# Chunk 0's score masking shared out between ScalarE, GpSimd and VectorE in a gated-linear-attention plus MLP kernel

## The chip, the core and the metric

The kernel runs on one core of a Trainium2 chip. A core has five engines that each work through their own list of instructions in order: TensorE (PE in the profile; its weight loads are shown apart as PEld), VectorE (DVE), ScalarE (ACT), GpSimd (POOL) and SyncE (SP, which here only issues DMAs). They wait for each other through semaphores. Matmul results land in PSUM, of which this kernel uses six banks of 512 numbers per partition and two tiles of sums; VectorE and ScalarE read them there, and GpSimd is given operands in SBUF only. The metric is the device time of one execution in microseconds, lower is better.

## The reference

```python
for t in range(S):                                   # q, k, v, alpha: (4, 8, 768, 48)
    state = alpha[:, :, t, :, None] * state + np.einsum('bhd,bhe->bhde', k[:, :, t], v[:, :, t])
    y[:, :, t] = np.einsum('bhd,bhde->bhe', q[:, :, t], state)
x = y.transpose(0, 2, 1, 3).reshape(B, S, H * D)     # (4, 768, 384)
xn = (x - mean(x)) / sqrt(var(x) + 1e-6) * g_ln      # over the last axis
out = x + maximum(xn @ w_ch1, 0) @ w_ch2             # 384 -> 1536 -> 384
```

A recurrence over 768 steps with a decaying 48x48 state per head is followed by a normalisation and a two-layer perceptron. All of it is single precision.

## The kernel before, in words

The sequence of each of the 4 batch entries is cut into 6 chunks of 128 steps. For one chunk of one entry (one "turn letter": a, b, c, d are chunk 0 of entries 0 to 3, e to h chunk 1, and so on to x) `attention(c, b)` does the following in pieces: logarithm of the gates (L296), running sums by a matmul with a triangle (L300), exponentials of both signs (L307, L308), scaled keys and queries (L314, L317), then transposes. In chunk 0 the transposes are matmuls (L334) whose results ScalarE copies out of PSUM (L338), queries first and keys second. The scores are matmuls (L368) with keys on the partitions and queries along the free axis, into two banks of 4 heads each, 128x512. They have to be masked: a key may only serve a query that is not earlier. Before the change VectorE does that with two `copy_predicated` per entry (L383), which write to the tile `at` only where the triangle `mask` is not zero; `at` was cleared beforehand. There are two tiles `at`, one for the even and one for the odd entries. The masked scores then meet the values (L427), beside the chunk's sum of outer products (L401) that becomes the state (L412). The outputs are summed and normalised on ScalarE: L454 copies them out of PSUM with their sum, L472 to L476 work out mean and spread, L478 and L479 apply them, L485 (PE) transposes, L489 (ACT) copies the result to `xT0`.

For chunk 0 the perceptron runs in plain single precision: first layer L520 on PE and L523 on ACT, two entries at a time, second layer L534. It needs the normalised rows of entries a and b (both L489) and the weights. In this data set the weights arrive as 64-bit numbers, and `take_weights` turns each of 12 pieces into single precision in VectorE and ScalarE steps: L186, L188, L190 (DVE), L194 (ACT, which waits for L190), L196 and L200 or L203 (DVE, which wait for L194). For the later chunks the weights are split in two parts (L213 to L219), and the products run as three cheaper ones (L557, L564, L623).

Nothing decides at run time what comes next. The string `ORDER` has one letter for each piece of each generator (a piece ends at a `yield`): a to x are the attention turns, A to L the weight pieces, Y and Z the first layer of chunk 0, and so on. Reading it from left to right gives each engine its list of instructions, and each engine keeps to its list. An instruction whose input isn't there holds up all that stands behind it on its engine.

```python
with tc.manual_schedule():
    for turn in ORDER:
        next(turns[turn], None)
```

Of the kernel before, what the change touches and what calls it, by code (L numbers as in the profile page):

```python
# [17 lines left out]
AFT = mybir.ActivationFunctionType  # L18
AOP = mybir.AluOpType
# [7 lines left out]
LOW = 2.0 ** -12  # L27

ORDER = (
    "NNNabaMMMNaaaaWVcbbbMccaaaabbbbbVccaaabbdcccbccddAAdWadaAaadbcccdbVbbBWVaaaddaabWNdccddb"  # L30
    "bbCbacddBBDVbbcCCddcddddeddYYDDYYYYeYWcccYcWWddYYEYYYYccYENNNFFEMWOF%ZWZeZZZZeZGZZZZZZZe"
    "eeGHYHGZZZZZZZZYMYYYZY%IeZWIHgeWJIfYWYYPJJg!Vffffee?OfffgeeKQ(LKMKMLL*gggOO#e.g!&fQQQQQQ"
    "?!!h+Q)eefege#eef&fffhhe.PPff(eNQQ%g//V#hh#eNe&eefffff&ieeffM+hhhf*PPPfffP*)ggggiiif%+PV"
    "M+j?i?ii-11211P((21133))gg1422-3i5P441115/h11523423N5N43gg5hhhhh4667-66ikk5gg6Vghh..gggg"
    "h*hiihhhhhhO-Ojii/MNji6jjjjj77ggk7h7Mggh7hh888881111821mmkkk3kjk2231131O444551122O113425"
    "Vll573366j66445iiii5N66ijjjjjk7ViijMkjlllliikkkkkjjj7iijjjjllii7ij7jjVnlmjmmN718888111Mm"
    "22m88111133442231554k5onkkmkkllllll2kkkk111OOm73V233N444M5566k66576lknnnnllnolll6mnmmm77"
    "ookklllllll88877V11pp188N111o223311n44M55OmO22mmmm33n4m5mm4666nnnpp57omm1112mnn12poo33n4"
    "4566m856nnnnVnn777npmmmnnVon88pnn7788111118223314qNM12N5N211334445N2oooqooqpp55q11q66ooo"
    "r23oo4opppp7pp1M6Mppp563oooo4566poqq8qoorrppp7o77pppVpp7pOV7Orrrrr118s888882123u1111142q"  # L40
    "34356115123445q66252qqqqq3sNss13tt46rqqqssqq4rrrVrrrqqqqM7tssrr556O6rqq7rrrrrOqu7qvtt7tt"
    "strrrr7r711888V881121112M334223N5sssvss14455ssss3ssuutttttss7458uusuu1t66t111wNs26233445"
    "5tt7MMO666stttt8tVt7V7ttsOtt88t7ss788vvvvO11111v122133x24211153344455u51166622336uuuu4ww"
    "vO478u55uuvuuvvvv67uuuV6vvwwwuwvvMvvv7vv7uuuuvvvv77w888xxxx88V11111122xx33O2314441155122"
    "5x3311263644ww64wwww7555ww66wwxxxxxwwwwxx7xx6xx7xxx7wxxxxOOwww7788888811111221O133442231"
    "31142555112663364447555866677777888888"
)


# [1 line left out]
def kernel(  # L51
# [17 lines left out]
    nc = tc.nc  # L69
# [4 lines left out]
    P = 128  # L74
    NCB = S // P
    NP = H // 2
# [39 lines left out]
    act, ts = nc.scalar.activation, nc.vector.tensor_scalar  # L116
    stt = nc.vector.scalar_tensor_tensor

    def rd(x):
        return x.bitcast(F32R)  # L120

    HS = P // 2
# [4 lines left out]
    mask, mask_of_halves = tri.bitcast(INT32), consts[:, 2 * P:].bitcast(INT32)  # L127
    nc.gpsimd.memset(consts[:, :2 * P], 1.0)
    nc.gpsimd.affine_select(out=tri, in_=tri, pattern=[[1, P]], base=0, channel_multiplier=-1,
                            compare_op=AOP.is_ge, fill=0.0)  # L130
    nc.gpsimd.affine_select(out=ident, in_=ident, pattern=[[1, P]], base=0, channel_multiplier=-1,
                            compare_op=AOP.is_equal, fill=0.0)
# [3 lines left out]
    def at_first(name, then):  # L136
# [20 lines left out]
    hh, hl, hs = (hid[:, i * NJ * HB * P:][:, :NJ * HB * P].rearrange(  # L157
        "p (j b t) -> p j b t", b=HB, t=P) for i in range(3))
# [131 lines left out]
    def attention(c, b):  # L290
        whole, last = c == 0, c + 1 == NCB
# [34 lines left out]
        at = ats[b % len(ats)]  # L326
        if not whole:
            at = at_parts[b % len(ats)][0].rearrange("k (p s t) -> k p s t", s=2, t=HS)
# [13 lines left out]
        else:  # L342
            nc.vector.transpose(out=tr.rearrange("t n i p d -> t (n i p) d"),
                                in_=qk.rearrange("t n i p d -> t (n i p) d"))
# [35 lines left out]
        give_kq(kT)  # L380
        yield
        for i, scores in enumerate(aps):
            nc.vector.copy_predicated(  # L383
                out=at[:, :, i].rearrange("k p s t -> k p (s t)") if whole else
                at.rearrange("k p s t -> k (p s) t"),
                data=scores.rearrange("k p s t -> k p (s t)" if whole else "k p s t -> k (p s) t"),
                mask=mask.unsqueeze(1).broadcast_to([P, NP, P]) if whole else
                mask_of_halves.unsqueeze(1).broadcast_to([P, 2 * NP, HS]))
            give_bank(scores)
        yield  # L390
        gate = gate_tile(P, 2, NP)
        with nc.allow_non_contiguous_dma(reason="two rows to columns"):
            nc.sync.dma_start(gate[:, :ne], line[:ne].rearrange("o (p r) -> r o p", p=NP))
# [248 lines left out]
    turns = {"YZ"[h]: first_of_chunk_0(h) for h in range(2)}  # L642
    turns |= {"PQ"[h]: second_of_chunk_0(h) for h in range(2)}
    turns |= {chr(ord("a") + n): attention(n // B, n % B) for n in range(NCB * B)}
    turns |= {t: take_weights(i) for i, t in enumerate("ABCDEFGHIJKL")}
    turns |= {t: split_weights(i) for i, t in enumerate("!#?%&()*+-./")}
# [35 lines left out]
```

## Time and profile before

| | |
|---|---|
| median of 3 runs | 405.09 us (404.27 to 408.36) |
| the profiled execution | 405.11 us, of it 403.4 us span of the core |
| TensorE busy | 396.5 us of the span (98%) |
| VectorE busy | 264.5 us (66%) |
| ScalarE busy | 251.2 us (62%) |
| GpSimd busy | 121.6 us (30%) |
| copy_predicated, all 28 (8 of them chunk 0's, 128x512 each) | median 732 ns |

How to read it: an engine at 98% leaves the question of where its other 2% are, and what stands behind them. The view by windows tells busy time stage by stage, the chain of waits tells what released what, and the timeline gives single instructions with their start, length and, in brackets, the idle time ahead of them with the engine and line that ended it. A name such as L338 is a line of the kernel before; `x2` behind a row means that two equal instructions were merged into it.

### The profile page before, as it was taken

How to read it: one execution, taken by the hardware profiler on the slowest of the kernel's cores; microseconds unless marked ns; L12 is line 12 of the kernel's file. 1: busy time of each engine (PE TensorE's matmuls, PEld its weight loads, DVE VectorE, ACT ScalarE, POOL GpSimd, SP SyncE). 2: the span in 40 equal slices, each digit the busy share in tenths (PEclk: the TensorE clock that was granted, in tenths of full speed). 3: DMA queues.
4: the chain of work that ended last, by engine and by line, in shares of the span. 5: the costliest groups of instructions: out<-in, count | busy, mean ns of one | idle time of the engine just before them, and what ended most of it. 6: DMA issues, size and time to landing. Idle time of an engine off the chain costs nothing.

```text
span 403.4 us, 12267 instructions
## 1 busy us (share of the span) xinstructions
PE 396.5 (98%) x5000; PEld 366.8 (91%) x5000; DVE 264.5 (66%) x468; ACT 251.2 (62%) x562; POOL 121.6 (30%) x129
## 2 busy tenths in 40 slices
PE   8999999999999999999999999999999999999996
PEld 6778886667999999999999999999999999999996
DVE  4898999989996665564564665575563664661461
ACT  5797655688884755674673774773575566556440
POOL 3010000023462442082352362352064171152170
PEclk9999999999999999999999999999999999999999
DMA  7888787767747837565456637748547715533101
GB/s 229 247 264 286 253 200 222 195 155 166 184 127 180 198 116 168 107 189 104 144 114 209 112 103 165 170 109 175 134 85 231 165 29 135 130 64 99 59 2 39
DMA packets 134240, 61.15 MB, mean 152 GB/s; under 512 B 90876, under 2 KB 130300, under 8 KB 134184
## 3 DMA queue, kind: packets, MB, share of 16 engines
q1 hardware_dynamic: 134184, 60.37, 58.9%
q8 instruction: 39, 0.64, 0.7%
q14 instruction: 17, 0.14, 0.1%
HBM read 42.95 MB, written 17.39 MB: 150 GB/s over the span
## 4 chain that ended last, share of the span: by engine, by line
PE 96%; ACT 1%; DVE 1%; issue 0%; DVEq 0%
PE bank L623 32%; PE bank L564 20%; PE bank L557 10%; PE bank L520 8%; PE bank L534 8%; PE bank L375 4%; PE bank L432 3%; PE sums L401 2%; PE bank L435 2%; PE bank L485 2%; PE bank L230 1%; PE bank L284 1%; PE bank L368 1%; PE bank L300 1%; PE bank L427 1%; PE bank L334 0%
## 5 line engine op out<-in xcount | busy, mean ns | idle before, releaser
L610 POOL TENSOR_TENSOR hid<-hid 128x512 fp32r<-128x512 f32 x60 | 76.1, 1291 | 63.9 <-DVE hid L602 59.7
L564 PE MATMUL bank<-xh,w1h 128*128 128x256 f32 x360 | 85.2, 278 | 0.0
L564 PE MATMUL bank<-xl,w1l 128*128 128x256 f32 x360 | 84.8, 276 | 0.0
L623 PE MATMUL bank<-w2h,hid 128*128 128x384 f32 x240 | 83.0, 346 | 0.0
L623 PE MATMUL bank<-w2l,hid 128*128 128x384 f32 x240 | 80.6, 336 | 0.0
L576 ACT ACTIVATE at<-bank 128x512 f32<-128x512 f32 x60 | 36.2, 604 | 60.3 <-PE bank L557 58.9
L584 DVE SCALAR_TENSOR_TENSOR bank<-bank,at 128x512 f32<-128x512 f32 x60 | 41.5, 696 | 41.5 <-PE bank L564 35.8
L564 PEld LDWEIGHTS bank<-xh,w1h 128*128 128x128 f32 x360 | 67.6, 188 | 0.2
L564 PEld LDWEIGHTS bank<-xl,w1l 128*128 128x128 f32 x360 | 67.6, 188 | 0.0
L557 PE MATMUL bank<-xs,ws 128*128 128x256 f32 x360 | 50.9, 277 | 0.0
L557 PEld LDWEIGHTS bank<-xs,ws 128*128 128x128 f32 x360 | 46.1, 188 | 0.3
L623 PEld LDWEIGHTS bank<-w2h,hid 128*128 128x128 f32 x240 | 45.1, 188 | 0.6
L623 PE MATMUL bank<-ws,hid 128*128 128x384 f32 x240 | 45.4, 336 | 0.0
L602 DVE SCALAR_TENSOR_TENSOR hid<-bank,hid 128x512 fp32r<-128x512 f32 x60 | 39.7, 683 | 8.5 <-ACT hid L594 8.2
L623 PEld LDWEIGHTS bank<-w2l,hid 128*128 128x128 f32 x240 | 45.1, 188 | 0.2 <-DVE hid L602 0.2
L419 POOL TENSOR_TENSOR mid<-mid,gate 112x192 f32<-112x192 f32 x20 | 11.0, 552 | 107.9 <-DMA kqT<-td 50.2
L623 PEld LDWEIGHTS bank<-ws,hid 128*128 128x128 f32 x240 | 41.6, 188 | 0.2
L593 ACT ACTIVATE hid<-bank 128x512 fp32r<-128x512 f32 x60 | 36.3, 605 | 8.3 <-DVE bank L584 8.0
L500 POOL TENSOR_TENSOR xs<-xs,xl 128x384 fp32r<-128x384 f32 x20 | 21.4, 1078 | 53.9 <-DVE xl L497 53.9
L594 ACT ACTIVATE hid<-bank 128x512 fp32r<-128x512 f32 x60 | 36.7, 611 | 0.0
L520 PE MATMUL bank<-early_hid,w 128*128 128x256 f32 x144 | 32.1, 382 | 0.0
L534 PE MATMUL bank<-w,early_hid 128*128 128x384 f32 x96 | 32.1, 489 | 0.0
(101 smaller groups left out, 784.7 us busy)
## 6 DMA issues: line engine op xcount, KB each, us to landing
early_w2l<-in_moe_w_ch_dram SPq DMA_DIRECT2D x12, 768.0 KB
td<-tr SPq DMA_DIRECT2D x80, 96.0 KB
kqT<-td SPq DMA_DIRECT2D x80, 96.0 KB
row<-in_alpha_dram SPq DMA_DIRECT2D x24, 192.0 KB
qk<-in_k_dram SPq DMA_DIRECT2D x24, 192.0 KB
qk<-in_q_dram SPq DMA_DIRECT2D x24, 192.0 KB
vn<-in_v_dram SPq DMA_DIRECT2D x24, 192.0 KB
kept<-row SPq DMA_DIRECT2D x24, 192.0 KB
```

Source lines behind the costliest of these rows:

```text
L500: nc.gpsimd.tensor_sub(rd(diff), diff, low)
L520: nc.tensor.matmul(hps, pieces[j // 2][0][:, f, j % 2 * P:][:, :P], xT0[:, f, bs], start=(f == 0), stop=(f == NF - 1))
L534: nc.tensor.matmul(ops, hT0[:, j, b], wholes[NT + j // 2][:, j % 2], start=(j == 0), stop=(j == NJ - 1))
L557: nc.tensor.matmul(hpb[:, i], rd(wj[i * NF + f][2]), rd(xv[f][2]), start=(f == 0), stop=(f == NF - 1))
L564: nc.tensor.matmul(hpa[:, i], rd(wj[i * NF + f][e]), rd(xv[f][e]), start=(f == 0 and e == 0), stop=(f == NF - 1 and e == 1))
L576: act(out=negs[t % len(negs)], in_=hpb, func=AFT.Copy, scale=-1.0)
L584: stt(out=z, in0=z, scalar=1 + LOW, in1=negs[t % len(negs)], op0=AOP.mult, op1=AOP.add)
L593: act(out=rd(high), in_=z, func=AFT.Relu, scale=1 - LOW / 2)
L594: act(out=rd(diff), in_=z, func=AFT.Relu, scale=LOW * (1 - LOW / 2))
L602: stt(out=rd(low), in0=z, scalar=0.0, in1=high, op0=AOP.max, op1=AOP.subtract)
L610: nc.gpsimd.tensor_sub(rd(diff), diff, low)
L623: nc.tensor.matmul(acc, rd(x[:, j, i]), rd(of[k][:, j % 2]), start=j == 0 and k != 1, stop=j == NJ - 1 and k != 0)
```

## The change

In chunk 0 the scores of an entry are treated by halves of the queries (HS is 64). The first 64 queries can only see the first 64 keys, so ScalarE copies that 64x64 corner of each head, unmasked, from PSUM to `at` (two instructions per entry, each 64 partitions by 4x64). GpSimd then clears what lies on the wrong side of the diagonal, with one `affine_select` per entry on 64x8x64 elements in SBUF. VectorE's `copy_predicated` stays for the other 64 queries, two per entry, each 128x4x64 in place of 128x4x128. The later chunks are as before.

```diff
-    "NNNabaMMMNaaaaWVcbbbMccaaaabbbbbVccaaabbdcccbccddAAdWadaAaadbcccdbVbbBWVaaaddaabWNdccddb"
+    "NNNabaMMMNaaaaWVcbbbMccaaaabbbbbVccaaabbdcccbccddAAdWadaAaadbccccdbVbbBWVaaaddaabWNdcc"
...
         for i, scores in enumerate(aps):
+            if whole:
+                act(out=at[:HS, :, i, 0], in_=scores[:HS, :, 0], func=AFT.Copy)
             nc.vector.copy_predicated(
-                out=at[:, :, i].rearrange("k p s t -> k p (s t)") if whole else
-                at.rearrange("k p s t -> k (p s) t"),
-                data=scores.rearrange("k p s t -> k p (s t)" if whole else "k p s t -> k (p s) t"),
-                mask=mask.unsqueeze(1).broadcast_to([P, NP, P]) if whole else
+                out=at[:, :, i, 1] if whole else at.rearrange("k p s t -> k (p s) t"),
+                data=scores[:, :, 1] if whole else scores.rearrange("k p s t -> k (p s) t"),
+                mask=mask[:, HS:].unsqueeze(1).broadcast_to([P, NP, HS]) if whole else
                 mask_of_halves.unsqueeze(1).broadcast_to([P, 2 * NP, HS]))
             give_bank(scores)
         yield
+        if whole:
+            first = at[:HS].rearrange("k p i s t -> k (p i) s t")[:, :, 0]
+            nc.gpsimd.affine_select(out=first, in_=first, pattern=[[0, 2 * NP], [1, HS]], base=0,
+                                    channel_multiplier=-1, compare_op=AOP.is_ge, fill=0.0)
+            yield
```

The new `yield` gives each chunk-0 turn one piece more. ORDER gets one letter more for each of a, b, c and d, right behind the piece that masks, so that all other pieces keep their places; nothing moves on PE or SP. In the changed file the new lines are L384 (the copy), L385 (copy_predicated) and L394 (the selection), and each line behind them has a number higher by 6.

On ScalarE, in the stretch of entries a and b (kqT_85 and kqT_86 are first a's and then c's transposed queries and keys, kqT_87 and kqT_88 are b's, at_175 belongs to a and at_176 to b), the list changes like this:

```order
 L338 COPY kqT_86<-bank_71 112x512
 L338 COPY kqT_87<-bank_66 112x512
+L384 ACTIVATE at_175<-bank_68 64x4x64
+L384 ACTIVATE at_175<-bank_70 64x4x64
 L338 COPY kqT_88<-bank_67 112x512
 L296 ACTIVATE row_75<-row_75 128x384
 L338 COPY kqT_85<-bank_69 112x512
+L384 ACTIVATE at_176<-bank_71 64x4x64
+L384 ACTIVATE at_176<-bank_66 64x4x64
 L338 COPY kqT_86<-bank_68 112x512
```

The copies of a's scores now stand between the copy of b's queries and the copy of b's keys, and those of b's scores between c's queries and c's keys.

On ScalarE a little later, where b's output is normalised, the changed kernel has these rows (L460 is L454 of before; kqT_88 is now entry d's keys, at_176 takes d's scores; L478 to L485 are L472 to L479 of before, for entry b):

```order
L460 ACTIVATE row_72,few_96<-bank_68 128x384
L338 COPY kqT_88<-bank_70 112x512
L384 ACTIVATE at_176<-bank_69 64x4x64
L384 ACTIVATE at_176<-bank_71 64x4x64
L478 ACTIVATE few_96<-few_96 128x1
L479 ACTIVATE row_74,few_96<-row_72,few_96 128x384
```

Before, L472 stood right behind the copy to kqT_88; now the two copies of d's scores stand between them, and d's scores can only be computed once kqT_88 is there.

On VectorE the changed kernel's masking of a and b, with the engines on whose semaphores each row waits:

```order
L385 COPY_PREDICATED at_175<-consts,bank_68 128x4x64 [waits Activation_49,Pool_49]
L385 COPY_PREDICATED at_175<-consts,bank_70 128x4x64 [waits Activation_49]
L385 COPY_PREDICATED at_176<-consts,bank_71 128x4x64 [waits PE_49,Activation_49]
L385 COPY_PREDICATED at_176<-consts,bank_66 128x4x64 [waits PE_49,Activation_49]
L186 TENSOR_SCALAR w_122<-early_w2l 128x768 [waits DMAHW3_49]
```

The masking instructions keep their place on VectorE, ahead of the first weight piece, and their lists of waits name ScalarE (Activation), which now reads the same bank ahead of them.

More of the change, by code (lines that the diff above doesn't have):

```diff
@@ L29 @@
 ORDER = (
-    "NNNabaMMMNaaaaWVcbbbMccaaaabbbbbVccaaabbdcccbccddAAdWadaAaadbcccdbVbbBWVaaaddaabWNdccddb"
[L31 to L46, printed above, removed]
+    "NNNabaMMMNaaaaWVcbbbMccaaaabbbbbVccaaaabbdcccbbccddAAdWadaAaadbccccdbVbbBWVaaaddaabWNdcc"
@@ new lines @@
+    "dddbbbCbacddBBDVbbcCCddcddddeddYYDDYYYYeYWcccYcWWddYYEYYYYccYENNNFFEMWOF%ZWZeZZZZeZGZZZZ"
+    "ZZZeeeGHYHGZZZZZZZZYMYYYZY%IeZWIHgeWJIfYWYYPJJg!Vffffee?OfffgeeKQ(LKMKMLL*gggOO#e.g!&fQQ"
+    "QQQQ?!!h+Q)eefege#eef&fffhhe.PPff(eNQQ%g//V#hh#eNe&eefffff&ieeffM+hhhf*PPPfffP*)ggggiiif"
+    "%+PVM+j?i?ii-11211P((21133))gg1422-3i5P441115/h11523423N5N43gg5hhhhh4667-66ikk5gg6Vghh.."
+    "ggggh*hiihhhhhhO-Ojii/MNji6jjjjj77ggk7h7Mggh7hh888881111821mmkkk3kjk2231131O444551122O11"
+    "3425Vll573366j66445iiii5N66ijjjjjk7ViijMkjlllliikkkkkjjj7iijjjjllii7ij7jjVnlmjmmN7188881"
@@ new lines @@
+    "11Mm22m88111133442231554k5onkkmkkllllll2kkkk111OOm73V233N444M5566k66576lknnnnllnolll6mnm"
+    "mm77ookklllllll88877V11pp188N111o223311n44M55OmO22mmmm33n4m5mm4666nnnpp57omm1112mnn12poo"
+    "33n44566m856nnnnVnn777npmmmnnVon88pnn7788111118223314qNM12N5N211334445N2oooqooqpp55q11q6"
+    "6ooor23oo4opppp7pp1M6Mppp563oooo4566poqq8qoorrppp7o77pppVpp7pOV7Orrrrr118s888882123u1111"
+    "142q34356115123445q66252qqqqq3sNss13tt46rqqqssqq4rrrVrrrqqqqM7tssrr556O6rqq7rrrrrOqu7qvt"
+    "t7ttstrrrr7r711888V881121112M334223N5sssvss14455ssss3ssuutttttss7458uusuu1t66t111wNs2623"
@@ L47 @@
+    "34455tt7MMO666stttt8tVt7V7ttsOtt88t7ss788vvvvO11111v122133x24211153344455u51166622336uuu"
+    "u4wwvO478u55uuvuuvvvv67uuuV6vvwwwuwvvMvvv7vv7uuuuvvvv77w888xxxx88V11111122xx33O231444115"
+    "51225x3311263644ww64wwww7555ww66wwxxxxxwwwwxx7xx6xx7xxx7wxxxxOOwww7788888811111221O13344"
+    "223131142555112663364447555866677777888888"
 )
```

## The prediction, made before the changed kernel was run

> **What bounds the kernel now.** I read the page first: TensorE's share and its row of slices.
>
> ```profile
> span 403.4 us, 12267 instructions
> ...
> PE 396.5 (98%) x5000; PEld 366.8 (91%) x5000; DVE 264.5 (66%) x468; ACT 251.2 (62%) x562; POOL 121.6 (30%) x129
> ...
> PE   8999999999999999999999999999999999999996
> ```
>
> A tenth of the span is 40 us, a digit 10 us. TensorE is full from the fourth digit on; what it lacks lies at the two ends. The view by windows shows the front end in us:
>
> ```profile
> 10.00:20.00 10.00, 9.42 (x167) 7.83 (x165) 8.64 (x16) 7.35 (x19) 0.00 (x0) 1.00 0.89 246
> 20.00:30.00 10.00, 9.21 (x138) 7.80 (x138) 9.79 (x18) 9.20 (x26) 1.05 (x2) 1.00 0.80 270
> ...
> 80.00:240.00 160.00, 160.00 (x2403) 151.31 (x2396) 107.84 (x194) 107.99 (x242) 61.24 (x62) 1.00 0.63 150
> ```
>
> Columns are the window, its length, then busy us of PE, PEld, DVE, ACT and POOL. From 10 to 30 us PE lacks 1.37 us, while VectorE and ScalarE are close to full; from 80 to 240 us PE lacks nothing. The view of waits, for PE alone from 60 us to the end, has a single row:
>
> ```profile
> PE sums L401 <- issue: 0.2, 1, 0.2
> ```
>
> So once PE has begun its dense run it waits for nobody, and the kernel's time is the time at which that run begins, plus a fixed length. What sets the beginning is in the chain of waits (start, length, what):
>
> ```profile
> 15.74 0.57 DVE early_w2l L190
> ...
> 16.34 0.99 ACT early_w2l L194
> 17.33 0.48 ACT row L454 x2
> ...
> 20.03 0.72 ACT row L479
> ...
> 20.80 0.55 PE bank L485 x3
> ...
> 25.90 4.12 PE bank L520 x18
> ```
>
> VectorE's weight step L190 releases ScalarE's L194, behind it ScalarE normalises entry a (L454 to L479), and PE's L485 comes from that. The dense run is L520, from 25.9 us. It matters less what the change saves on VectorE, then, than what it does to ScalarE's and VectorE's lists ahead of 25.9 us. I follow these, as shifts against the profiled execution. TensorE's rows there:
>
> ```profile
> 10.45 2.14 PE L368 MATMUL bank<-kqT,kqT 48*128 48x128 f32 x32
> 12.51 1.09 PE L334 MATMUL bank<-consts,early_w2h 128*112 128x128 f32 x8
> ...
> 20.80 0.55 PE L485 MATMUL bank<-consts,row 128*128 128x128 f32 x3 [0.85 <-ACT row L479]
> ...
> 21.77 1.16 PE L368 MATMUL bank<-kqT,kqT 48*128 48x128 f32 x16
> ...
> 24.29 0.55 PE L485 MATMUL bank<-consts,row 128*128 128x128 f32 x3
> ...
> 25.87 4.15 PE L520 MATMUL bank<-early_hid,w 128*128 128x256 f32 x18
> ```
>
> and ScalarE's:
>
> ```profile
> 10.27 0.61 ACT L338 COPY kqT<-bank 112x512 f32<-112x512 f32 x1
> 10.75 0.62 ACT L338 COPY kqT<-bank 112x512 f32<-112x512 f32 x1
> ...
> 13.24 0.59 ACT L338 COPY kqT<-bank 112x512 f32<-112x512 f32 x1 [1.45 <-issue]
> ...
> 21.11 0.57 ACT L338 COPY kqT<-bank 112x512 f32<-112x512 f32 x1
> 21.57 0.21 ACT L472 ACTIVATE few<-few 128x1 f32<-128x1 f32 x1
> ...
> 25.34 0.47 ACT L489 COPY early_hid<-bank 128x384 f32<-128x384 f32 x1
> ...
> 32.27 0.64 ACT L523 ACTIVATE early_hid<-bank 128x256 f32<-128x256 f32 x2
> ```
>
> and VectorE's:
>
> ```profile
> 11.71 2.57 DVE L383 COPY_PREDICATED at<-consts,bank 128x512 f32<-128x512 int32 x4 [1.25 <-PE bank L368]
> 14.17 0.55 DVE L186 TENSOR_SCALAR w<-early_w2l 128x768 int32<-128x768 int32 x1
> 14.75 0.96 DVE L188 SCALAR_TENSOR_TENSOR w<-early_w2l,w 128x768 f32<-128x768 uint32 x1
> ...
> 18.40 1.28 DVE L200 SCALAR_TENSOR_TENSOR w<-w,small,early_w2l 128x256 f32<-128x256 f32 x3
> ```
>
> **Prices of the parts.** Eight ScalarE copies of 64x(4x64) are added. No row has this shape; per partition it is 256 elements from PSUM, as in L523: two take 0.64 us, so one 0.36 us and a follower 0.28 us later. I take 0.28 us for each in the queue; the bound above is L338's pace at twice the elements, 0.48 us (10.27 to 10.75), the bound below half of that, 0.24. The eight L383 shrink to half: now four take 2.57 us, 0.62 us apart (14.17 - 11.71 = 2.46 us for four). At 256 elements I take 0.35 us, between half (0.31) and L200's pace at 256 elements (0.40). VectorE is spared about 8 x 0.27 = 2.1 us. Four GpSimd selections are added, of 512 elements on 64 partitions:
>
> ```profile
> 2.04 0.29 POOL L129 TENSOR_SCALAR_AFFINE_SELECT consts<-consts 128x128 f32<-128x128 f32 x1
> ...
> 23.60 0.52 POOL L466 MEMSET at<- 128x512 f32 x1 [19.55 <-PE bank L427]
> ...
> L610 POOL TENSOR_TENSOR hid<-hid 128x512 fp32r<-128x512 f32 x60 | 76.1, 1291 | 63.9 <-DVE hid L602 59.7
> ```
>
> A selection of 128 elements takes 0.29 us. With 512 elements I bound it by the memset of 512 (0.52) and the two-operand L610 (1.29); four times L129 would be 1.16. I take 0.87, 0.10 us fixed and four times the remaining 0.19; the row it is nearest to is L129.
>
> **Step 1, b's keys wait behind a's scores: +1.5 us on PE.** On ScalarE the copies of a's scores now stand ahead of the copy of b's keys (10.75 us). They need a's scores, which VectorE saw at 11.71. So they go at 11.71 and 11.99, the key copy at 12.27 in place of 10.75, and it ends at 12.89. The 32 rows of L368 are a's 16 and b's 16, each half of 12.51 - 10.45, 1.03 us; b's began at 11.48 and now begin at about 12.94. L334 for entry c goes from 12.51 to 13.97.
>
> **Step 2, VectorE waits for b's copies: +2.1 us.** ScalarE's copy of c's queries (13.24, released by that L334) moves by the same 1.46 to 14.70. Behind it come the copies of b's scores, at 15.18 and 15.46, the second done at 15.82. The order shows that each `copy_predicated` waits for ScalarE; b's two run at 15.58 and 15.93, and L186 starts at 16.28 in place of 14.17. Queued behind them on VectorE are all three of L186, L188 and L190, and L194 on ScalarE waits for the last of them: 16.34 becomes 18.45. VectorE's saving of about 1.1 us on these four is gone in this wait. c's second L338 copy (behind b's) ends near 16.3, ahead of PE, which needs it for c's scores at 15.60 + 1.46 = 17.06.
>
> **Step 3, c's copies inside the normalising of a: +0.56 us.** They stand between L454 and L472 in the chain above, with their scores long there (17.06 + 1.1). L479 goes from 20.03 by 2.11 + 0.56 to 22.70, PE's L485 from 20.80 to 23.47, +2.67.
>
> **Step 4, d's copies wait for d's scores: +1.96 us.** Before, L472 followed 0.46 us behind the copy of d's keys (21.11). Now that copy is at 23.78, ends at 24.35; L368 for d goes from 21.77 to 24.44 and its 1.16 us end at 25.60, and only then do the copies start, at 25.62 and 25.90. L472 of entry b comes at 26.20 in place of 21.57: +4.63. This is a round trip ScalarE to PE to ScalarE on an engine that never waited there.
>
> **Step 5, to the dense run.** From L472 on ScalarE's list is as before and was unbroken up to the second L489 at 25.34, which released L520 at 25.87 (L485 of b, 24.29, becomes 28.92; PE idles some 1.9 us ahead of it). So L520 begins at 25.87 + 4.63 = 30.50.
>
> **What is hidden.** The selections lie beside other work. a's scores are copied by 12.35, so its selection ends at 13.2, and PE wants `at` at 16.0:
>
> ```profile
> 14.57 1.10 PE L427 MATMUL bank<-vn,at 128*64 128x48 f32 x32
> ...
> 24.76 1.14 PE L427 MATMUL bank<-vn,at 128*64 128x48 f32 x32
> ```
>
> (14.57 + 1.46). d's ends at 27.1, wanted at 24.76 + 4.63 = 29.39. A selection would have to last over 3 us to be seen. DMAs issued on SP behind PE, ScalarE or VectorE move by less than 4.63, and so do the weight pieces: the second piece's L196 waits for the L194 between the two L489, and ends up 3.4 us later than before, so PE, 4.6 us later, finds its weights with more slack than now. Nothing behind 30.5 us gives time back, since PE waits for nothing there.
>
> **Sum**: 1.46 + 0.65 (steps 1 and 2) + 0.56 + 1.96 = 4.63 us. The profiled execution's own time is 405.11, 1.7 us over its span, and 0.02 from the median of 405.09. 405.11 + 4.63 = 409.74, say 409.8. With all eight copies on this path at 0.24 or at 0.48 us in place of 0.28 the sum goes from 4.3 to 6.2.
>
> **Rival 1, GpSimd shuts VectorE out: 410.2.** The trace shows that the two can block each other:
>
> ```profile
> 248.16 1.01 POOL L500 TENSOR_TENSOR xs<-xs,xl 128x384 fp32r<-128x384 f32 x1 [4.73 <-DVE xl L497]
> ...
> 248.46 1.13 DVE L317 TENSOR_TENSOR qk<-qk,eq 128x384 f32<-128x384 f32 x1
> ...
> L317 DVE TENSOR_TENSOR qk<-qk,eq x20: 544/551/1134, 48.0 to 343.4; 128x384 f32<-128x384 f32 x20
> ```
>
> L317's median is 0.55 us (last row: shortest, median, longest in ns); beside L500 it takes 1.13 and ends 0.42 us after it. Here b's selection starts at 15.86 and lasts to 16.73, just where L186 should start at 16.28. If L186 is shut out, it and L194 lose 0.45 us more: 410.2; with a selection of 1.29 us 0.87, so 410.6. L186 reads one SBUF operand, L317 two, and no row shows L186 beside GpSimd; only L188, at 16.86, would be hit for certain, and only by a selection over 1.0 us. The Trainium skill, SBUF — State Buffer, section "SBUF: two separate sides", says that a VectorE operation in a two-port mode too is excluded for the whole of a GpSimd instruction. The trace agrees for L317; by that rule L186 is hit, since at 0.55 us for the elements on which L188 spends 0.96 it looks like such a mode.
>
> **Rival 2, part of the delay is absorbed: 407.8.** If d's scores are copied without the round trip of step 4 costing ScalarE its place, only 2.67 us remain. Against it: strict order on ScalarE, as the [1.45 <-issue] ahead of L338 at 13.24 shows.
>
> **Rival 3, VectorE's relief wins: 404.1.** The chain runs over L190. If a's copies found ScalarE idle (it has 1.45 us ahead of 13.24), and b's keys were not behind them, L190 would come 4 x 0.27 = 1.1 us earlier, and so would L194 and the dense run: 405.11 - 1.1 = 404.0 to 404.1. It decides at one point, whether the key copy still starts before a's scores are ready at 11.71; in the order it doesn't.
>
> **Rival 4, PE slows after its longer stalls: 412 or more.** PE's clock is not the same everywhere, though the granted clock reads 1.00:
>
> ```profile
> 1.12 3.78 PE bank L230 x16
> ...
> 8.49 0.87 PE bank L334 x8
> ```
>
> The same 128 columns take 236 ns at first and 109 later. If the 1.9 us of step 5 threw PE back, half of L520's first 4.15 us at that rate would cost 2 us and more: 411.8 to 414. Against it: the 0.85 us of idleness ahead of L485 at 20.80 did not; the 16 rows of L368 behind it take 73 ns each. The Trainium skill, TensorE: Matmul & The Clock Gate, Part 1, wants about 3.4 us of idleness for the slow state; by that rule it stays fast.
>
> **How the numbers follow.** 1% of 405.09, about what a measurement of this kernel can tell from no change, is 4.05 us: slower begins at 409.14. Forecast as summed 0.42, rival 1 0.28, rival 2 (and anything else that eats 1 to 3 us) 0.19, rival 4 0.07, rival 3 0.04. A tenth of the forecast's weight may fall below 409.14. So slower 0.73, within 1% 0.23, faster 0.04. The range goes from rival 2 to the dear end of the copies (411.3) with some of rival 1: 407.8 to 411.6.
>
> **What would show it.** In the profile after: the key copy of b at 12.3, not 10.8; idle PE ahead of L368 and L485; ScalarE waiting for L368 ahead of d's copies; L186 at 16.3 (16.7 for rival 1); L520 at 30.5; from there on the same dense run. It is wrong if L520 starts before 29.5, or if PE waits after it.

## The result, and the profile after

| | before | after |
|---|---|---|
| median | 405.31 us (404.27 to 408.36, 4 runs) | 410.85 us (409.51 to 411.79, 4 runs) |
| ratio | 1 | 1.0119, 95% interval 1.0078 to 1.016 |
| the profiled execution | 405.11 us, span 403.4 | 410.34 us, span 408.6 |
| TensorE busy | 396.5 us | 397.2 us |

The changed kernel is slower by 5.5 us, 1.2%. VectorE's part shrank as meant: the view of its masking line in the profile after has the eight chunk-0 instructions at 256 elements.

```profile
L385 DVE COPY_PREDICATED at<-consts,bank x28: 430/732/748, 11.4 to 367.5; 128x512 f32<-128x512 int32 x20, 128x256 f32<-128x256 int32 x8
```

Now the same stretch as in the prediction. First TensorE's timeline in the profile after (start, length, instruction, and in brackets the idle time ahead of it and what ended it):

```profile
9.66 1.16 PE L368 MATMUL bank<-kqT,kqT 48*128 48x128 f32 x16
12.07 1.16 PE L368 MATMUL bank<-kqT,kqT 48*128 48x128 f32 x16 [1.25 <-ACT kqT L338]
13.17 1.09 PE L334 MATMUL bank<-consts,early_w2h 128*112 128x128 f32 x8
...
18.80 0.65 PE L334 MATMUL bank<-consts,early_w2h 128*112 128x128 f32 x4 [1.38 <-DVE early_w2h L317]
...
22.68 0.55 PE L491 MATMUL bank<-consts,row 128*128 128x128 f32 x3 [1.23 <-ACT row L485]
...
28.05 0.65 PE L491 MATMUL bank<-consts,row 128*128 128x128 f32 x3 [1.81 <-ACT row L485]
28.64 1.95 PE L433 MATMUL bank<-vn,at 128*64 128x48 f32 x32
...
30.52 4.75 PE L526 MATMUL bank<-early_hid,w 128*128 128x256 f32 x18
```

PE, whose longest pause in this stretch was 0.85 us, now has four waits of 1.2 to 1.8 us. What they wait for is in ScalarE's and VectorE's timelines of the same profile:

```profile
10.90 0.65 ACT L384 ACTIVATE at<-bank 64x256 f32<-64x256 f32 x2 [0.81 <-issue]
11.45 0.57 ACT L338 COPY kqT<-bank 112x512 f32<-112x512 f32 x1
...
13.89 0.59 ACT L338 COPY kqT<-bank 112x512 f32<-112x512 f32 x1 [1.45 <-issue]
14.38 0.65 ACT L384 ACTIVATE at<-bank 64x256 f32<-64x256 f32 x2
...
17.85 0.99 ACT L194 ACTIVATE early_w2l<-early_w2l,small 128x768 int32<-128x768 int32 x1 [1.48 <-DVE early_w2l L190]
...
19.72 0.20 ACT L478 ACTIVATE few<-few 128x1 f32<-128x1 f32 x1
...
23.00 0.58 ACT L338 COPY kqT<-bank 112x512 f32<-112x512 f32 x1
24.89 0.65 ACT L384 ACTIVATE at<-bank 64x256 f32<-64x256 f32 x2 [1.32 <-issue]
25.44 0.19 ACT L478 ACTIVATE few<-few 128x1 f32<-128x1 f32 x1
...
29.16 0.46 ACT L495 COPY early_hid<-bank 128x384 f32<-128x384 f32 x1
```

```profile
11.38 0.77 DVE L385 COPY_PREDICATED at<-consts,bank 128x256 f32<-128x256 int32 x2 [1.71 <-ACT at L384]
14.79 0.79 DVE L385 COPY_PREDICATED at<-consts,bank 128x256 f32<-128x256 int32 x2 [2.63 <-ACT at L384]
15.46 0.76 DVE L186 TENSOR_SCALAR w<-early_w2l 128x768 int32<-128x768 int32 x1
```

The reader sees three waits that weren't there: ScalarE 0.81 us for a's scores with b's key copy queued behind, VectorE 2.63 us for ScalarE's copies of b with the weight piece queued behind, and ScalarE 1.32 us for d's scores with b's normalising queued behind.

The last two rows of the TensorE view show something else. L433 for entry d took 1.95 us; the same 32 rows took 1.14 before. The view by windows of the profile after, by its column for the granted clock (the last figure but two), shows why:

```profile
24.94:28.35 3.41, 1.60 (x51) 1.48 (x48) 2.96 (x5) 3.25 (x11) 1.52 (x2) 1.00 1.00 326
28.35:31.77 3.42, 3.42 (x38) 2.87 (x37) 2.45 (x5) 3.36 (x10) 0.53 (x1) 0.50 0.31 90
```

Behind a stretch in which PE was busy for only 1.60 of 3.41 us, its clock was granted at half for 3.42 us, and the beginning of the dense run fell into that. In the chain of waits the run's first 18 rows took 4.68 us, where they had taken 4.12:

```profile
28.71 1.88 PE bank L433 x32
30.59 4.68 PE bank L526 x18
```

Behind 31.8 us all is as before: PE waits for nobody to the end but once for 0.3 us (before: once for 0.2).

The mean granted clock is known for every execution, not only for the profiled ones. A half-clock stretch of 3.42 us lowers it by 0.004 over a span of 408 us; the last 1.2 to 1.3 us of the span, behind all work on PE, also read 0.50 in both profiles, so values from 0.998 up need no stretch in the work. The four executions of the changed kernel had 0.994, 0.995, 0.995 and 0.991. Of the 43 executions of the kernel before that ran beside the experiments, 31 had 0.998 or more and took 404.2 to 406.0 us, and 12 had 0.992 to 0.996 and took 406.8 to 409.5. So PE's clock drops in the kernel before too, only less often, and the profile before shows an execution in which it didn't.

### The profile page after: what moved, and what is told of

It is laid out like the page before. It is cut to its first block, busy times and chain, and to the rows that moved or that the text cites. A ratio compares the mean times of both kernels' runs of the same rounds, so it can differ in the third digit from the quotient of the medians.

```text
span 408.6 us, 12284 instructions
## 1 busy us (share of the span) xinstructions
PE 397.2 (97%) x5000; PEld 367.6 (90%) x5000; DVE 264.0 (65%) x468; ACT 253.5 (62%) x570; POOL 125.9 (31%) x133
## 4 chain that ended last, share of the span: by engine, by line
PE 94%; ACT 2%; DMA 1%; DVE 1%; issue 1%; SPq 0%
PE bank L629 31%; PE bank L570 20%; PE bank L563 10%; PE bank L526 8%; PE bank L540 8%; PE bank L375 4%; PE bank L438 3%; PE bank L441 2%; PE sums L407 2%; PE bank L491 2%; DMA gate<-line 1%; PE bank L230 1%; PE bank L284 1%; PE bank L433 0%; PE bank L300 0%
## 5 line engine op out<-in xcount | busy, mean ns | idle before, releaser
L425 POOL TENSOR_TENSOR mid<-mid,gate 112x192 f32<-112x192 f32 x20 | 12.3, 613 | 106.0 <-DVE mid L423 93.9
L526 PE MATMUL bank<-early_hid,w 128*128 128x256 f32 x144 | 32.5, 385 | 0.0
```

The source lines that it names most:

```text
L526: nc.tensor.matmul(hps, pieces[j // 2][0][:, f, j % 2 * P:][:, :P], xT0[:, f, bs], start=(f == 0), stop=(f == NF - 1))
```

## The experiments

The entries a, b, c and d are those of the prediction. Ratios are against runs of the kernel before on the same chip; its median was 405.40 us on one chip and 405.45 on the other.

**The changed kernel without the selections.**

```diff
         if whole:
             first = at[:HS].rearrange("k p i s t -> k (p i) s t")[:, :, 0]
-            nc.gpsimd.affine_select(out=first, in_=first, pattern=[[0, 2 * NP], [1, HS]], base=0,
-                                    channel_multiplier=-1, compare_op=AOP.is_ge, fill=0.0)
             yield
```

> The changed kernel without the four GpSimd selections, so the first 64 queries of chunk 0 stay unmasked: that part of the masking is left out. Theory (ScalarE's copies stand in the wrong places of its list, GpSimd is a side matter): L186 goes back from 0.76 to 0.55 us and the time falls by 0.2 us only, to 410.6 against 405.3 before, ratio about 1.013. Rival (GpSimd keeping VectorE out makes up most of the loss): the time falls by 2 us or more, below 409, ratio under 1.009.

Measured: 410.46 us, ratio 1.0104 (1.0037 to 1.017). GpSimd is a side matter. What it did cost is seen in VectorE's timeline; first the profile after, GpSimd's selection for b, then L186 of this run:

```profile
15.16 0.65 POOL L394 TENSOR_SCALAR_AFFINE_SELECT at<-at 64x512 f32<-64x512 f32 x1 [2.89 <-ACT at L384]
```

```profile
16.14 0.55 DVE L186 TENSOR_SCALAR w<-early_w2l 128x768 int32<-128x768 int32 x1
```

Without a selection beside it L186 takes 0.55 us. In the profile after it started at 15.46, inside the selection's 15.16 to 15.81, and took 0.76. So the exclusion of rival 1 applies to this one-operand instruction too, and costs it 0.21 us; a gain that small can't be told in the time. The Trainium skill, SBUF — State Buffer, section "SBUF: two separate sides", has the exclusion for a VectorE operation in a two-port mode; no run here shows whether L186 is in one. L200 is hit in the same way in the profile after: beside the selection for c its three instructions took 1.76 us, and 1.28 in this run.

**Entry d masked as before.** The new form is limited to the other entries; d gets the whole `copy_predicated` back:

```diff
+        split = whole and b in (0, 1, 2)
         for i, scores in enumerate(aps):
-            if whole:
+            if split:
                 act(out=at[:HS, :, i, 0], in_=scores[:HS, :, 0], func=AFT.Copy)
...
+            else:
+                nc.vector.copy_predicated(
+                    out=at[:, :, i].rearrange("k p s t -> k p (s t)") if whole else
...
-        if whole:
+        if whole and not split:
+            yield
+        if split:
             first = at[:HS].rearrange("k p i s t -> k (p i) s t")[:, :, 0]
```

> The changed kernel in which entry d alone is masked as before (two whole copy_predicated, no copies, no selection). Theory (step 4: ScalarE waits for d's scores before it goes on to normalise b): the 1.32 us of waiting and the two copies are gone, L526 starts 2 us earlier, PE's wait ahead of the second L491 falls to near nothing and the clock stays up: 407.5, ratio 1.005. Rival (the copies cost what ScalarE works, wherever they stand, 0.28 us each): only 0.6 us are gained, 410.3, ratio 1.012.

Measured: 407.43 us, ratio 1.0025 (0.9989 to 1.0061), 3.4 us below the changed kernel. In this run's ScalarE timeline the round trip is gone:

```profile
23.80 0.57 ACT L338 COPY kqT<-bank 112x512 f32<-112x512 f32 x1
24.26 0.21 ACT L486 ACTIVATE few<-few 128x1 f32<-128x1 f32 x1
```

The first row of b's normalising follows the key copy after 0.46 us, where in the changed kernel it was 2.44 (23.00 to 25.44). So 2.0 us of the 3.4 are step 4. The rest may be the clock, though no run separates it: seven of the ten executions here had 0.998 or more, and none of the changed kernel's four. The clock fell in the profiled execution as well, but between 19.8 and 23.3 us, where it stretched a wait and not the dense run:

```profile
20.00:22.50 2.50, 2.50 (x45) 2.16 (x45) 2.46 (x5) 2.40 (x11) 0.95 (x1) 0.50 0.97 311
```

**The same instructions, a's and b's copies moved.** Only the order of the turns is changed: b's second copy and b's scores go ahead of the masking of a, and b's masking ahead of c's first copy.

```diff
-    "NNNabaMMMNaaaaWVcbbbMccaaaabbbbbVccaaaabbdcccbbccddAAdWadaAaadbccccdbVbbBWVaaaddaabWNdcc"
+    "NNNabaMMMNaaaaWVcbbbMccaaaabbbbbVccabbaaadccbbcccddAAdWadaAaadbccccdbVbbBWVaaaddaabWNdcc"
```

> The changed kernel with the same instructions, and only ORDER changed: b's second key copy and b's scores come ahead of the masking of a, and the masking of b ahead of c's query copy. Theory (steps 1 and 2 are a matter of place): the copies of a and b fall into ScalarE's idle time of 1.45 us, PE's waits ahead of b's scores (1.25) and of the second L334 (1.4) go, L186 starts 2 us earlier, and 2.1 to 2.4 us are gained: 408.5, or 407.5 if the clock stays up too, ratio 1.005 to 1.008. Rival (it is the added work, not its place): same time as the changed kernel within 0.5 us, ratio 1.012 to 1.0135.

Measured: 408.27 us, ratio 1.0057 (1.0018 to 1.0096). The ScalarE row of b's copies and VectorE's row of L186 in this run:

```profile
12.52 0.65 ACT L384 ACTIVATE at<-bank 64x256 f32<-64x256 f32 x2
```

```profile
13.60 0.76 DVE L186 TENSOR_SCALAR w<-early_w2l 128x768 int32<-128x768 int32 x1
```

The copies lie in what was ScalarE's idle time, and L186 starts earlier than in the kernel before (14.17). So steps 1 and 2 are a matter of place; the work is the same. The ten executions lie between 405.89 and 410.63 us, though, and their times follow the clock: three at 0.998 or more took 405.89 to 406.92, five at 0.992 to 0.995 took 407.74 to 409.95, and two at 0.986 took 410.62 and 410.63. The profiled one, 409.95, shows a half-clock stretch of twice the length in its windows:

```profile
22.80:26.21 3.41, 1.60 (x53) 1.38 (x49) 2.85 (x6) 3.00 (x10) 1.53 (x2) 1.00 1.05 355
26.21:33.04 6.83, 6.83 (x45) 5.60 (x46) 5.73 (x10) 6.67 (x18) 0.53 (x1) 0.50 0.44 109
```

**PE kept busy in its waits.** Matmuls of zeros, into a tile of sums that holds zeros, ahead of the first two L491:

```diff
+WARM = 8, 12
...
+        if whole and b < 2:
+            for _ in range(WARM[b]):
+                nc.tensor.matmul(sums[1].rearrange("r p d -> r (p d)")[:, :P], zero[:, :R], zero,
+                                 start=True, stop=True)
         xps = bank(P, NF, P)
```

> The changed kernel with 8 matmuls of zeros on PE ahead of L491 of entry a and 12 ahead of L491 of entry b, into a tile of sums that holds zeros; they should end inside PE's waits of 1.2 and 1.8 us there. Theory (the granted clock of 0.92 and 0.91 between 20 and 40 us comes from PE's idle time and costs 1.4 us: L433 of d took 1.95 us where it took 1.14 before, the first 18 rows of L526 4.68 where 4.12): the clock stays near 1.00 there, the two rows are as before, and the time falls by 1.4 us to about 409.4, ratio 1.010. Rival (the slow rows have another cause than PE's idle time): the clock reads 0.91 to 0.92 again and the time stays at 410.8, ratio 1.0135.

Measured: 410.34 us, ratio 1.0105 (1.0024 to 1.0185): the expected gain didn't show in the time. The trace tells both halves. The clock read 1.00 throughout the profiled execution (another of the four had 0.994 and took 412.01 us), and L433 and the dense run had their old pace; but the matmuls ran over. In this run's timeline (L492 are the zeros, L496 is L491 of the changed kernel):

```profile
27.26 2.88 PE L492 MATMUL sums<-early_hid 128*112 128x128 f32 x24
29.97 0.49 PE L496 MATMUL bank<-consts,row 128*128 128x128 f32 x3
30.39 1.14 PE L434 MATMUL bank<-vn,at 128*64 128x48 f32 x32
31.46 2.86 PE L531 MATMUL bank<-early_hid,w 128*128 128x256 f32 x12
```

ScalarE had its part ready at 29.09 (28.38 and 0.71), and L496 began 0.88 us later; ahead of the first L496 it was 0.38 us. In the changed kernel L491 follows after 0.04, so some 1.2 us were given back. Hence a shorter version, with `WARM = 4, 6`:

> The changed kernel with 4 and 6 matmuls of zeros in PE's two waits ahead of L491 in place of 8 and 12, which ran 0.35 us and about 0.7 us over the ends of the waits. Theory (half clock after PE's idle time): the granted clock stays at 1.00 in the stretch from 20 to 40 us, nothing runs over, and the time is that of the changed kernel less 1.0 to 1.4 us: 409.4 to 409.8, ratio 1.010. Rival (the clock is not the cause, or half as many matmuls don't hold it): 410.8, ratio 1.0135, with a stretch at 0.50.

Measured: 409.12 us, ratio 1.0094 (1.0074 to 1.0114), 1.7 us below the changed kernel, with all six executions between 408.75 and 410.10. Four of them had a clock of 1.00 and took 408.75 to 409.20; two had 0.996 and took 410.08 and 410.10. In the profiled execution, 410.08, the dense run began at full clock. A half-clock stretch came earlier instead, from 14.1 to 17.5 us, behind PE's wait of 1.25 us ahead of b's scores, which nothing fills:

```profile
14.50:17.00 2.50, 2.50 (x9) 1.49 (x7) 1.02 (x3) 1.60 (x4) 0.65 (x1) 0.50 0.78 263
```

**Both together**, the moved order and the 4 and 6 matmuls:

> The order with the copies of a and b moved (all four entries split, 408.3 with executions from 405.9 to 410.6), plus the same 4 and 6 matmuls of zeros. Theory (that spread is the half clock falling or not falling on the dense run): the executions lie closer together and the median falls to 407.3 or below, ratio 1.004, the clock at 1.00 throughout. Rival (the spread has another cause): median 408.3 and a spread of 4 us or more as without the matmuls.

Measured: 407.23 us, ratio 1.0043 (1.0025 to 1.0062), seven executions between 406.40 and 407.95: a spread of 1.6 us where the same order without the matmuls had 4.7. Its windows:

```profile
10.00:20.00 10.00, 9.48 (x170) 8.22 (x169) 7.75 (x17) 8.52 (x25) 2.22 (x3) 1.00 0.90 255
20.00:30.00 10.00, 9.26 (x144) 7.96 (x143) 8.32 (x17) 8.35 (x23) 2.06 (x3) 1.00 0.74 237
30.00:40.00 10.00, 10.00 (x50) 8.02 (x50) 9.52 (x17) 8.96 (x26) 0.00 (x0) 1.00 0.85 256
```

The medians alone (408.27 and 407.23) don't separate the two, since their intervals overlap. The spread and the clock do: all seven executions had 0.999 or 1.00, where only three of ten had 0.998 or more without the matmuls. The gain is in the executions that the half clock had made long; the three without it took 405.89 to 406.92 as they were.

**Only a and b in the new form, in the moved order.** This puts the change where ScalarE has room and leaves c and d alone.

> Only entries a and b are masked in the new way, and in the order that fits ScalarE's idle time (b's second key copy and b's scores ahead of the masking of a, b's masking ahead of c's query copy); c and d are masked as before. Theory (the cost was place alone): no wait is added, L186 starts 0.5 us earlier than before, less about 0.2 for GpSimd beside it, the clock stays at 1.00: 405.1, ratio 0.999. Rival (the added copies cost 0.28 us each wherever they are): 406.5, ratio 1.003.

Measured: 405.30 us, ratio 0.9996 (0.9963 to 1.0029): no difference from the kernel before, with half of the new copies and selections in it. In both sets of executions some had the lower clock (4 of 12 here, 7 of 24 of the kernel before). Work for ScalarE was not the cost. In VectorE's timeline L186 has its short duration; it began 0.12 us before b's selection (12.88 to 13.53) ended, so GpSimd cost nothing here either:

```profile
13.41 0.56 DVE L186 TENSOR_SCALAR w<-early_w2l 128x768 int32<-128x768 int32 x1
```

**VectorE's relief alone**, no copies and no selections:

```diff
-            if whole:
-                act(out=at[:HS, :, i, 0], in_=scores[:HS, :, 0], func=AFT.Copy)
...
-            nc.gpsimd.affine_select(out=first, in_=first, pattern=[[0, 2 * NP], [1, HS]], base=0,
-                                    channel_multiplier=-1, compare_op=AOP.is_ge, fill=0.0)
```

> The changed kernel with neither the ScalarE copies nor the GpSimd selections: the scores of the first 64 queries of chunk 0 are left out. It shows what VectorE's shorter masking alone would give (rival 3 of the prediction). Theory: VectorE's four halved instructions ahead of L186 bring L186 and L194 1.05 us forward, ScalarE's chain follows, L526 starts 1 us earlier than in the kernel before: 404.4, ratio 0.9975. Rival (another wait takes its place at once, the transposes of d or a DMA): 405.4, ratio 1.000.

Measured: 405.09 us, ratio 0.9994 (0.996 to 1.0028): the rival's number; a gain of 1 us would be inside the interval, but the trace of the profiled execution (405.13) shows that it had none. Its VectorE and TensorE rows:

```profile
11.71 0.78 DVE L383 COPY_PREDICATED at<-consts,bank 128x256 f32<-128x256 int32 x2 [1.25 <-PE bank L368]
12.71 0.78 DVE L383 COPY_PREDICATED at<-consts,bank 128x256 f32<-128x256 int32 x2 [0.23 <-PE bank L368]
13.59 0.56 DVE L186 TENSOR_SCALAR w<-early_w2l 128x768 int32<-128x768 int32 x1
```

```profile
20.25 0.55 PE L487 MATMUL bank<-consts,row 128*128 128x128 f32 x3 [0.83 <-ACT row L481]
...
24.28 0.56 PE L403 MATMUL sums<-vn,early_w2h 128*48 128x48 f32 x16 [0.83 <-DVE w L186]
...
26.32 4.15 PE L522 MATMUL bank<-early_hid,w 128*128 128x256 f32 x18
```

VectorE now waits for b's scores, so L186 comes 0.58 us earlier, not 1.05. PE's first row here is L485 of before (20.80) and comes 0.55 us earlier too. Then L403 for entry d waits 0.83 us, and the dense run starts at 26.32, later than the 25.87 of before. The row names L186, a weight step that L403 doesn't read; L403 needs the state step ahead of it on VectorE, which was over at 22.6, and d's values, whose transfer was issued at 18.9. The trace also has the landing: the last part of that transfer arrived at 24.14, and PE's wait for its semaphore ended at 24.17. So PE waited for a DMA. In the profile before, the same transfer was issued at 19.41 and had landed by 23.26; here it was issued earlier and landed later.

## Why the prediction was right, and where it was not

The range held the time and the sign was right; the size was forecast as +4.7 and measured as +5.5 us between medians. Step by step, with starts from the two profiled executions. In the one after, everything up to the first L307 was 0.79 us early; the table's fifth column takes that out. The two rows, before and after:

```profile
6.22 0.49 ACT L307 ACTIVATE eq<-bank 128x384 f32<-128x384 f32 x1 [1.90 <-PE bank L300]
```

```profile
5.43 0.49 ACT L307 ACTIVATE eq<-bank 128x384 f32<-128x384 f32 x1 [0.84 <-PE bank L300]
```

The four L300 on PE that end the wait took 2.24 us before and 1.46 after, with the same work. In the profiles of the eight experiments L307 begins anywhere between 5.56 and 6.22, so this is taken for a difference between executions.

| what | before | after | shift | shift + 0.79 | forecast |
|---|---|---|---|---|---|
| copy of b's keys (step 1) | 10.75 | 11.45 | 0.70 | 1.49 | 1.52 |
| L334 for c on PE (step 1) | 12.51 | 13.17 | 0.66 | 1.45 | 1.46 |
| L186 (step 2) | 14.17 | 15.46 | 1.29 | 2.08 | 2.11 |
| L194 (step 2) | 16.34 | 17.85 | 1.51 | 2.30 | 2.11 |
| L472, now L478, of a (step 3) | 17.83 | 19.72 | 1.89 | 2.68 | 2.67 |
| L472, now L478, of b (step 4) | 21.57 | 25.44 | 3.87 | 4.66 | 4.63 |
| second L489, now L495 (step 5) | 25.34 | 29.16 | 3.82 | 4.61 | 4.63 |
| dense run, L520, now L526 | 25.87 | 30.52 | 4.65 | 5.44 | 4.63 |

- **Steps 1 to 5 came out as worked out from the rows**, to 0.04 us but for L194. The price of the copies was right: two take 0.65 us, a pair holds the queue for 0.55. The experiments confirm what the steps are: moving a's and b's copies gave 2.6 us back, undoing d 3.4, both and c undone 5.5 (all with what the clock gave back beside it).
- **Step 2 lacked 0.2 us, rival 1's exclusion.** It was priced at 0.45 and given a chance of its own; it is real and measured 0.21, because the selection took 0.65 us and not 0.87, and because L186 ended only 0.41 us behind it, less than its own 0.55. Step 3 gave as much back: c's copies cost 0.38 instead of 0.56, since they cover a pause that L472 had before.
- **Rival 2 did not happen.** ScalarE waited out the whole round trip of step 4: 1.32 us of idle time ahead of d's copies at 24.89.
- **The term that was mis-sized is the last one, from ScalarE's second L489 to the dense run.** Rival 4, PE slowing after its stalls, had a chance of 0.07. It happened: L433 at half clock held PE back by 0.8 us, and the first rows of the dense run took another 0.56, some 1.4 us in all. "By that rule it stays fast" did not come true. The Trainium skill, TensorE: Matmul & The Clock Gate, Part 1, asks for an idle window of about 3.4 us. The trace agrees with the length (the half-clock stretch was 3.42 us, and twice that in the moved order), but not with the condition, since PE's longest idle piece was 1.8 us and it was busy for 1.60 of the 3.41 us ahead. That the 0.85 us of before did no harm was one profiled execution's evidence: in 12 of 43 others of that kernel the clock was lower.
- **That the dense run began at 30.52, forecast 30.50, is luck.** The early front took 0.79 us off and the half clock put 0.81 on. The profiled times differ by 5.23 us: 4.6 of waits, 1.4 of clock, less 0.8.
- **How the medians' 5.5 us divide is open.** All four executions of the changed kernel had the lower clock. The four executions with the shorter matmuls and a clock of 1.00 (408.75 to 409.20 us) lie 3.6 us above the median of the kernel before at 0.998 or more on the same chip (405.34), where the profile has 4.6 us of waits. The front of an execution without a profile isn't known, so what makes the difference isn't shown.
- **Rival 3 was over-priced.** VectorE's relief was put at 1.1 us on the way to the dense run. Alone it moved L186 by 0.58 and the time by nothing, since PE then waited for a transfer.
- **What was called hidden was hidden.** Each selection took 0.65 us beside other work, and PE waited for none of them. The weights were there: PE has no wait for VectorE behind 30.5 us.

## What to carry to other kernels

Work that an idle engine takes over costs what stands behind it in that engine's list, from the moment at which it starts to wait for its input: read the engine's list at the place of insertion, and ask for each instruction behind it who needs it. Eight copies of 0.3 us cost 4.6 us in one order, and four of them nothing in another. Behind new waits on TensorE, add the clock to the bill, and look for the half-clock stretch in the windows rather than for a long idle piece. Read the granted clock of every execution too: a single profile of a kernel can show the one in which it didn't drop.

## What the runs showed of the hardware that was not expected

- The granted clock of PE went to 0.50 for 3.42 us (28.35 to 31.77) behind a stretch of 3.41 us in which PE was busy for 1.60 us in pieces, with no idle piece over 1.8 us; in another run the same kind of stretch was followed by 6.83 us of half clock. In three more profiles PE was busy for 1.65, 2.03 and 2.16 us of the 3.41 ahead of a drop, and for 2.26 of 3.41 (21.53 to 24.94 in the profile after) without one behind it; no run was made to find a threshold. Where it falls differs between kernels, and whether it comes at all differs between executions of one kernel (12 of 43 of the kernel before). Matmuls of zeros in the waits took the spread from 4.7 to 1.6 us.
- A one-operand VectorE instruction (L186, 128x768) is held up by a GpSimd selection that runs when it starts: 0.76 us in place of 0.55, finishing 0.41 us behind the selection's end. Where it began 0.12 us before that end, it took 0.56.
- A GpSimd selection of 64x512 took 0.65 us, where one of 128x128 takes 0.29: 0.94 ns for each further element per partition. In the moved order, where it ran beside L200, the one for c took 0.95.
